# A transformer block on one core: a V tile moved behind transposes, rows normalised earlier, two lower pieces on another engine

## The chip, the cores and the metric

One core of a Trainium2 chip. The metric is device time in microseconds of one execution of the whole program, smaller is better; the median of several executions is quoted. Engines are TensorE (PE, with its weight loads PEld), VectorE (DVE), ScalarE (ACT), GpSimd (POOL) and SyncE (SP, which here only issues DMAs).

## The reference

An adaLN block over 2048 tokens of width 512 with 32 heads of 16, followed by an MLP of 1792:

```python
mod = (_silu(c) @ w_mod)                      # six rows of 512: sa, ca, ga, sb, cb, gb
h = _layernorm(x, axis=-1) * (1 + ca) + sa
qkv = h @ wqkv                                # 32 heads of 16
p = softmax(q k^T * scale)                    # 2048 x 2048 per head, no mask
x = x + ga * (p @ v) @ wo
h = _layernorm(x, axis=-1) * (1 + cb) + sb
x = x + gb * (gelu(h @ w1 + b1) @ w2 + b2)
```

All data are float32. The kernel keeps that precision by splitting each operand into an upper piece (rounded to fp32r) and a lower piece (the rest), and by multiplying three of the four products of pieces.

## The kernel before

**Order.** The kernel is scheduled by hand: each engine executes its instructions in the order in which the program emits them, and waits at an instruction until its inputs are there. A DMA is issued by the engine that the program names (`sy` is SP, `ac` is ScalarE), in that engine's order. The DMAs of both issuers share eight landing semaphores in rotation, so that an issue waits until the transfer that last used its semaphore has landed.

**First part (0 to about 83 us).** The tokens are four blocks of 512, each four tiles of 128 rows. `first_block` (L306) does block 0 with an order of its own: transposes, modulation rows in two halves (`mod_part`, L202, two groups of eight matmuls each), `mod_copy` to SBUF, `mod_cols` (L218: small matmuls that turn the row into a column scale and shift, modc), then the key and query projections of feature group 0, written as "hh", "lh" and "hl" (upper-upper, lower weights, lower activations) per chunk of 128 features. `put`, `value` and `lower` make the upper piece on ScalarE, the value on ScalarE and the lower piece on VectorE. Then the loop `for b in range(NB)` (L626) does, for each b: for b > 0 the statistics of block b + 1 (`ln1`, L271); the key projection of block b (`proj_qk`, w = 1); the query projection (w = 0); for b = 0 the statistics and rows of block 1; `V_A[b][0]` V tiles (`proj_v`, L470: 128 rows of V, 12 matmuls, one ScalarE evacuation, one store); the transposes of block b + 1 and their evacuation (`ln1_t`, L283: ScalarE makes h with modc, VectorE the upper piece, VectorE and GpSimd in turn the lower); `V_A[b][1]` V tiles; modulation rows. In `ln1` the statistics (L239 to L244: VectorE, and a GpSimd power for the factor) come first and the rows (L281, four VectorE instructions) only when the returned function is called.

**Key sums.** For feature groups 0 and 1, `proj_qk` of an odd block also forms the sum and the difference of its keys with those of the block before (VectorE L447), their upper pieces (ScalarE L448) and lower pieces (L463), and stores them (L453). These sums (`kpm_d`) serve a cheap bound of the row maxima. What `proj` calls last, `rest`, is the stores of the operation before: they are emitted one operation late, behind the next operation's evacuation.

**Second part.** V tiles not done yet and feature groups 1 to 3 form a list of items (`items`). From item FILL0 on, their matmuls are interleaved with "visits", three slots of row-maxima matmuls each (`half_slot`, L551: matmul L565, ScalarE L571, VectorE L574), which need the key sums in SBUF: `build_k` (L496) loads them, six DMAs for blocks 0 and 1 in the pass b = 3 of the first loop, the rest at fixed items. PSUM is eight banks; `bank()` hands out banks 3 to 6 in rotation in the first part.

**Third part.** Attention: score matmuls L966 and exponentials L967 with the products with V (L799), row maxima of later heads beside them (L546, L548); then output projection and MLP to the end.

## Time and profile before

| | us |
|---|---|
| median of 3 runs | 1738.33 (1737.28 to 1740.88) |
| profiled execution | 1736.68 |
| its span, first to last instruction | 1734.9 |
| TensorE busy in the span | 1726.3 (100%) |
| VectorE, ScalarE, GpSimd busy | 1393.7, 1352.0, 319.2 |

Rows below give start and length in microseconds, engine, line, operation and what it writes and reads; "x8" counts instructions that are merged in one row, whose starts follow one another; a bracket gives the idle time of the engine in front and what ended it. Matmuls are pipelined, so that a group's length reaches beyond the start of the next, and a busy share near 100% is no proof of a full TensorE; starts are compared instead. The granted TensorE clock is full throughout the span.

### The profile page before, as it was taken

The page shows a single profiled execution, that of the slowest core. Times are in us where ns is not written, and L with a number is a line of the kernel's source. Part 1 is how long each engine was busy: PE and PEld are TensorE (multiplying, and loading weights), DVE is VectorE, ACT ScalarE, POOL GpSimd, SP SyncE. Part 2 cuts the span into 40 slices and gives each one's busy share as a digit, 9 for nine tenths or more (in the row PEclk, how much of TensorE's full clock was granted, in tenths as well). Part 3 has the DMA queues.
Part 4 walks back from the last instruction along what each step waited for, and adds up shares of the span by engine and source line. Part 5 has one row for each costly group of instructions (what it writes and reads, how often), then busy time and mean ns, then how long its engine had stood idle before and what let it go on. Part 6 is the DMA issues. An engine that isn't in the chain of part 4 may idle for free.

```text
span 1734.9 us, 28894 instructions
## 1 busy us (share of the span) xinstructions
PE 1726.3 (100%) x10560; PEld 898.1 (52%) x10560; DVE 1393.7 (80%) x2558; ACT 1352.0 (78%) x2582; POOL 319.2 (18%) x346
## 2 busy tenths in 40 slices
PE   9999999999999999999999999999999999999998
PEld 6755554443433343343443443433333488888887
DVE  6599999898888888888888888888885296746553
ACT  4488888999999999999999999999999632222222
POOL 3205431010000000000000000000013154635562
PEclk9999999999999999999999999999999999999999
DMA  9767667412201400500500110101023064423331
GB/s 319 224 136 183 156 134 149 96 48 45 54 23 40 68 21 23 85 23 24 87 25 23 39 36 23 39 26 33 23 65 103 21 204 126 139 77 115 98 121 49
DMA packets 125218, 144.15 MB, mean 83 GB/s; under 512 B 39026, under 2 KB 74866, under 8 KB 123124
## 3 DMA queue, kind: packets, MB, share of 16 engines
q1 hardware_dynamic: 121764, 135.55, 30.8%
q10 hardware_dynamic: 3312, 6.76, 1.0%
q8 instruction: 83, 1.36, 0.3%
q14 instruction: 59, 0.48, 0.1%
HBM read 106.37 MB, written 35.87 MB: 82 GB/s over the span
## 4 chain that ended last, share of the span: by engine, by line
PE 97%; DVE 2%; DMA 0%; POOL 0%; ACT 0%; issue 0%; ACTq 0%; POOLq 0%
PE pv L799 29%; PE mx L546 20%; PE sc L303 16%; PE sc L966 13%; PE mx L1030 6%; PE mx L565 5%; PE pv L1030 2%; PE sc L906 2%; PE mx L906 1%; PE sc L260 0%; PE pv L343 0%; DMA qk<-parts 0%; PE sc L356 0%; DVE xin L281 0%; PE sc L205 0%; DVE glo L1013 0%
## 5 line engine op out<-in xcount | busy, mean ns | idle before, releaser
L967 ACT ACTIVATE p<-sc 128x512 f32<-128x512 f32 x2048 | 1054.7, 613 | 38.1 <-PE sc L966 12.0
L548 DVE TENSOR_REDUCE mxs<-mx 128x1 f32<-128x512 f32 x1472 | 927.2, 683 | 112.8 <-PE sc L966 84.8
L799 PE MATMUL pv<-p,vg 128*32 128x512 f32 x4096 | 546.0, 605 | 0.0
L966 PE MATMUL sc<-qst,kq 50*128 50x512 f32 x1024 | 284.2, 435 | 0.0
L966 PE MATMUL sc<-qst,kt 50*128 50x512 f32 x1024 | 282.1, 431 | 0.0
L546 PE MATMUL mx<-kq,qmx 48*128 48x512 f32 x768 | 261.8, 428 | 0.2
L546 PEld LDWEIGHTS mx<-kq,qmx 48*128 48x128 f32 x768 | 122.5, 184 | 228.4 <-DVE mxs L548 209.3
L546 PE MATMUL mx<-kt,qmx 48*128 48x512 f32 x704 | 239.9, 427 | 0.0
L546 PEld LDWEIGHTS mx<-kt,qmx 48*128 48x128 f32 x704 | 113.4, 184 | 208.5 <-DVE mxs L548 190.7
L1009 ACT ACTIVATE g<-sc,b_c 128x512 f32<-128x512 f32 x56 | 38.6, 690 | 222.7 <-PE sc L303 218.2
L574 DVE CUSTOM_DVE_ANT_0 cp<-mx,cp 128x512 f32<-128x512 f32 x288 | 182.8, 687 | 21.2 <-PE mx L565 17.3
L587 POOL CAST m<-mn 128x16 fp32r<-128x16 f32 x32 | 6.3, 198 | 1012.0 <-DVE mn L581 1011.9
L571 ACT ACTIVATE cp<-mx 128x512 f32<-128x512 f32 x288 | 151.5, 602 | 29.7 <-PE mx L565 29.3
L799 PEld LDWEIGHTS pv<-p,vg 128*32 128x32 f32 x4096 | 81.1, 108 | 180.6 <-issue 168.9
L966 PEld LDWEIGHTS sc<-qst,kq 50*128 50x128 f32 x1024 | 125.5, 185 | 32.2 <-ACT p L967 23.7
L1013 DVE TENSOR_TENSOR glo<-g,ghi 128x512 fp32r<-128x512 f32 x56 | 57.6, 1028 | 92.2 <-ACT ghi L1012 92.2
L966 PEld LDWEIGHTS sc<-qst,kt 50*128 50x128 f32 x1024 | 125.6, 185 | 9.8 <-ACT p L967 3.1
L835 POOL TENSOR_TENSOR w1l<-w1r,w1h 128x512 fp32r<-128x512 f32 x56 | 76.5, 1366 | 146.7 <-DVE w1h L834 123.1
L565 PE MATMUL mx<-kt,qmx 48*128 48x512 f32 x576 | 100.5, 437 | 0.0
L837 POOL TENSOR_TENSOR w2l<-w2r,w2h 128x512 fp32r<-128x512 f32 x56 | 82.5, 1473 | 6.2 <-DVE w2h L836 5.8
L565 PEld LDWEIGHTS mx<-kt,qmx 48*128 48x128 f32 x576 | 54.4, 184 | 49.4 <-DVE mxf L574 24.5
L303 PE MATMUL sc<-kt,w1h 128*128 128x512 f32 x224 | 73.9, 391 | 0.0
(175 smaller groups left out, 1667.7 us busy)
## 6 DMA issues: line engine op xcount, KB each, us to landing
w1r<-in_B_w_dram SPq DMA_DIRECT2D x56, 256.0 KB
w2r<-in_B_w_dram SPq DMA_DIRECT2D x56, 256.0 KB
qk<-parts SPq DMA_DIRECT2D x25, 512.0 KB
qmx<-qk SPq DMA_DIRECT2D x192, 64.0 KB
qst<-qk SPq DMA_DIRECT2D x192, 64.0 KB
kq<-qk SPq DMA_DIRECT2D x24, 256.0 KB
kt<-qk SPq DMA_DIRECT2D x24, 256.0 KB
vg<-v SPq DMA_DIRECT2D x8, 664.0 KB
```

Source lines behind the costliest of these rows:

```text
L303: te.matmul(ps, p, q, start=i == 0, stop=i == len(terms) - 1)
L546: te.matmul(ps, qmx[u][rows, p, qc * P : (qc + 1) * P], kst[u // NB][rows, p, kr * TB : (kr + 1) * TB], start=True, stop=True)
L548: ve.tensor_reduce(mxs[u][:, p, a, qc, kr : kr + 1], ps, axis=AX.X, op=ALU.max, negate=True)
L565: te.matmul(ps, qmx[u][rows, p, qc * P : (qc + 1) * P], kpm[u // NB][rows, p, t0 : t0 + TB], start=True, stop=True)
L571: ac.activation(vabs[n, a], ps, AF.Abs)
L574: ve.tensor_tensor_reduce(v, ps, v, -0.5, 3.0e38, ALU.add, ALU.min, mxs[u][:, p, a, qc, r : r + 1])
L799: te.matmul(cur_pv[0][32 * j : 32 * (j + 1)], vg[g][:, kc, j * VW : j * VW + 32], pt.pop((s, j)), start=kc == 0, stop=kc == NKC - 1)
L835: gp.tensor_tensor(alo, a, ahi.bitcast(F32), op=ALU.subtract)
L837: gp.tensor_tensor(blo, b, bhi.bitcast(F32), op=ALU.subtract)
L966: te.matmul(ps, k[r0 : r0 + KX, p, kc * P : (kc + 1) * P], q[r0 : r0 + KX, p], start=True, stop=True)
L967: ac.activation(pb, ps, AF.Exp, scale=SCALE)
L1030: te.matmul(acc[qb][t], p[:, sl], q, start=f == 0 and n == 0, stop=f == NF - 1 and n == 2)
```

## The change

- In `first_block`, the second modulation group is emitted before the second chunk's upper products, which move behind the copy of the modulation row; of the products with lower weights the first chunk's come before `mod_cols` and the second's behind it.
- `V_A[0]` is (3, 1): a fourth V tile is done in the pass b = 0, behind the transposes of block 1, and in front of the modulation rows. The remaining list of V tiles is one shorter; FILL0 and the item numbers at which loads are issued go down by one, so that they stay with the same V tile. The change of ScalarE's store queue to SP's at item 1 stays at item 1.
- `ln_stats` computes the factor for tiles 0 and 1, and for 2 and 3, separately.
- For b = 1 and 2 the rows of block b + 1 are normalised at once, in front of the key projection's evacuation.
- For b = 1 the stores of keys and key sums are emitted right behind the key projection, in front of the query projection.
- The lower pieces of block 0 and 1's key sums of group 0 are made by VectorE instead of GpSimd.

```diff
-FILL0 = 4
+FILL0 = 3
-V_A = ((3, 0), (1, 1), (0, 1))
+V_A = ((3, 1), (1, 1), (0, 1))
@@ ln_stats
+        rs = small.tile([P, 4], F32, tag="rs", name="rs")
         for t in range(4):
             ln_stat(mv, t, tiles[t])
-        rs = small.tile([P, 4], F32, tag="rs", name="rs")
-        ln_factor(mv, rs)
+            if t % 2:
+                ln_factor(mv, rs, t - 1, t + 1)
@@ first_block
         mm("hh", 0)
         mod_part(mod, 0, wms[0], HD, D)
-        mm("hh", 1)
         mod_part(mod, 1, wms[1], HD, D)
         value(0)
         mod_copy(mod, mrow, HD, D)
         value(1)
         lower(0)
-        mm("lh", 0, 1)
+        mm("hh", 1)
+        mm("lh", 0)
         mod_cols(0, mrow, cols, 2, 4)
+        mm("lh", 1)
         lower(1)
@@ proj_qk, rest
-                    eng = ve if not k and b == NB - 1 else gp
+                    eng = gp if k else ve
@@ for b in range(NB)
             if b + 1 < NB:
-                rows = ln1(b + 1)
+                xn = ln1(b + 1)()
...
-        elif b:
-            xn = rows()
+        elif b == 1:
+            rest()
+            rest = lambda: None
         proj(proj_qk, b, 0, 0, (), None if b else first[0])
@@ items
-        if 2 < n < 6:
-            build_k(kts[0], kpm_d[0], 0, 2 * TB, S, (n - 3,))
-        if n == 6:
+        if 1 < n < 5:
+            build_k(kts[0], kpm_d[0], 0, 2 * TB, S, (n - 2,))
+        if n == 5:
             load_w(2)
-        if n == 8:
+        if n == 7:
             build_k(kts[1], kpm_d[0], 1)
```

## The prediction

> **What bounds the kernel now.** First the page: its head, and the shares of the chain of work that ended last.

> ```profile
> span 1734.9 us, 28894 instructions
> ...
> PE 97%; DVE 2%; DMA 0%; POOL 0%; ACT 0%; issue 0%; ACTq 0%; POOLq 0%
> ```

> TensorE carries 97% of the chain, so a microsecond of TensorE idleness removed anywhere is worth one at the end, unless a later wait takes it back. The change touches the part before attention; there I read that chain in order of time, cut to 0–90 us.

> ```profile
> 25.57 6.75 DMA qk<-parts
> 32.40 0.34 ACTq L480
> ...
> 42.70 3.88 DVE xin L281 x4
> ...
> 48.26 2.80 PE sc L303 x12
> ...
> 70.64 12.33 PE sc L303 x52
> 82.97 0.66 PE mx L565 x3
> ```

> Columns are start, length, engine and line. In this stretch the chain leaves TensorE: a store of key pieces lands after 6.75 us, only then does ScalarE issue its next DMA (L480) and evacuate block 1's transposes (h); further on VectorE's row normalising (L281) holds block 2's. A V tile, 12 matmuls, is 2.80 us. From 70.64 it is TensorE alone: V tiles, then the first row-maxima matmuls (L565). What TensorE loses stands in its timeline:

> ```profile
> 30.58 1.51 PE L260 MATMUL mx<-ident,xin 128*128 128x128 f32 x12
> ...
> 32.46 1.92 PE L205 MATMUL sc<-wmod,s_m 128*32 128x512 f32 x16
> 34.31 2.02 PE L303 MATMUL sc<-hThi,w 128*128 128x512 f32 x6
> ...
> 39.22 2.00 PE L303 MATMUL sc<-hThi,w 128*128 128x512 f32 x8
> ...
> 45.66 2.16 PE L260 MATMUL mx<-ident,xin 128*128 128x128 f32 x12
> ...
> 48.02 2.11 PE L303 MATMUL sc<-wv,hThi 128*128 128x512 f32 x8
> ...
> 58.44 2.37 PE L260 MATMUL mx<-ident,xin 128*128 128x128 f32 x12
> ...
> 61.00 1.18 PE L303 MATMUL sc<-wv,hThi 128*128 128x512 f32 x4
> ```

> Matmul lengths overlap, so I take start to start. Block 1's key projection, also 12 matmuls, takes 39.22 − 34.31 = 4.91 where a V tile takes 2.80: **2.11 lost**, waiting for the evacuation of its transposes. Block 1's sixteen transposes take 32.46 − 30.58 = 1.88, block 2's 48.02 − 45.66 = 2.36 (**0.48 lost**), block 3's 61.00 − 58.44 = 2.56 (**0.68 lost**).

> **The change, part by part.** *Order of the first block.* The scale and shift of its last two chunks come through two modulation groups (L205), a copy and four small matmuls (L224).

> ```profile
> 14.99 0.73 PE L356 MATMUL sc<-hThi,w 128*128 128x512 f32 x2
> 15.66 0.64 PE L205 MATMUL sc<-wmod,s_m 128*32 128x256 f32 x8
> 16.23 1.20 PE L356 MATMUL sc<-hThi,w 128*128 128x512 f32 x4
> 17.26 0.50 PE L224 MATMUL pv<-sel,mrow 128*128 128x2 f32 x4
> ```

> The second group moves in front of two matmuls (15.66 − 14.99 = 0.67 earlier), and two of the four matmuls at 16.23 slip behind L224, (17.26 − 16.23) / 2 = 0.5. So L224 starts near 16.8 instead of 17.26, and the chain behind it (scale and shift, evacuation, lower piece, the next matmuls) follows up to 0.48 earlier. I take **0.35**, nearer the upper end since TensorE itself then becomes the limit; the lower end is 0 (the group's weights land later).

> *Fourth V tile.* It moves, 2.80 us with one ScalarE evacuation and one store, from in front of block 2's transposes to behind block 1's. The key projection then starts 2.80 − 0.35 after 34.31, at 36.8.

> ```profile
> 35.17 1.40 POOL L267 TENSOR_TENSOR hTlo<-h,hThi 128x512 fp32r<-128x512 f32 x1 [6.28 <-DVE hThi L266]
> 35.46 1.66 DVE L267 TENSOR_TENSOR hTlo<-h,hThi 128x512 fp32r<-128x512 f32 x1
> ...
> 37.05 0.41 DVE L266 CAST hThi<-h 128x512 fp32r<-128x512 f32 x1
> ```

> The last upper piece is there at 37.05 + 0.41 = 37.46 and is used by the seventh matmul, near 38.2. All **2.11** go. The list of V tiles shifts by one: three instead of four stand between block 3's projections and the first maxima visit, which stays in the eleventh V tile, since FILL0 and the item numbers fall by one.

> *Rows first, factor in halves, lower pieces on VectorE.* Each factor call gets one more VectorE instruction (0.17 and an estimated 0.1 of handover) and one more GpSimd power. Two GpSimd subtractions become two of VectorE.

> ```profile
> 28.92 1.92 DVE L281 TENSOR_SCALAR xin<-xin,mv,rs 128x512 f32<-128x512 f32 x4 [1.12 <-POOL rs L244]
> ...
> 40.77 0.68 DVE L441 TENSOR_TENSOR parts<-sc,parts 128x512 fp32r<-128x512 f32 x1
> ...
> 42.79 1.60 POOL L463 TENSOR_TENSOR pmh<-pm,pmh 128x512 fp32r<-128x512 f32 x1 [0.84 <-ACT pmh L448]
> ...
> 47.61 2.12 ACT L265 ACTIVATE h<-mx,modc 128x512 f32<-128x512 f32 x3 [0.74 <-PE mx L260]
> ...
> 55.52 0.17 DVE L243 TENSOR_SCALAR rs<-mv 128x4 f32<-128x4 f32 x1
> ...
> 58.64 0.60 ACT L440 ACTIVATE parts<-sc 128x512 fp32r<-128x512 f32 x1 [1.64 <-PE sc L303]
> ...
> 69.57 0.69 DVE L463 TENSOR_TENSOR pmh<-pm,pmh 128x512 fp32r<-128x512 f32 x1
> ```

> Four rows take 3.88 at 42.70, beside GpSimd's subtractions, and 1.92 at 28.92 without. VectorE in block 1 after the change: rows start where the key's lower piece did, 0.27 later, at 41.0, and end at 43.0; key lower piece and two sums, 42.70 − 40.77 = 1.93, to 44.9; two lower pieces of 0.69, to 46.3. Block 2's transposes come near 46.0 on TensorE and find their rows done: the **0.48** go. The price is on ScalarE. The stores of key and sums are now issued in front of the query's copy; behind the second sum's store (46.3) queue that copy (0.60), the query's lower piece on VectorE (0.68), the issue of its store and then h. With 0.34 an issue: 46.3 + 0.34 + 0.60 + 0.68 + 0.34 = 48.3, against 47.61: h **0.7 later**. The V tile behind the transposes takes the query's PSUM bank, free only at 47.9: a new TensorE wait, 0 to 0.4.

> The second power would run beside rows 0 and 1, as one does in the first block:

> ```profile
> 8.12 2.14 DVE L328 TENSOR_SCALAR xin<-xin,mv,rs 128x512 f32<-128x512 f32 x4
> ...
> 8.29 0.93 POOL L244 TENSOR_TENSOR rs<-rs,mhalf 128x2 f32<-128x2 f32 x1 [1.24 <-DVE rs L243]
> ```

> Four rows take 2.14 there instead of 1.92: 0.2 more, left to the range. [...]

> *Block 3.*

> ```profile
> 51.87 0.41 DVE L266 CAST hThi<-h 128x512 fp32r<-128x512 f32 x1
> ...
> 59.97 1.45 ACT L265 ACTIVATE h<-mx,modc 128x512 f32<-128x512 f32 x2 [0.74 <-PE mx L260]
> ...
> 65.07 1.28 POOL L267 TENSOR_TENSOR hTlo<-h,hThi 128x512 fp32r<-128x512 f32 x1 [1.42 <-DVE hThi L266]
> ```

> With h 0.7 later, block 2's last upper piece ends at 51.87 + 0.41 + 0.7 = 53.0; statistics and factor, which ended at 55.52 + 0.17, at 56.7; rows 1.92 later, at 58.6. Transposes want them from about 58.4: of 0.68 some 0.5 go. But the key's lower piece now stands behind the rows, to 59.3, and the issue of its store stands on ScalarE ahead of h: h near 59.7, against 59.97. So block 3's evacuation, and its last lower piece on GpSimd (65.07 + 1.28 = 66.35) that the key projection's last matmul uses, **stay about where they were**. TensorE arrives up to 0.4 sooner and waits.

> **What is late next.** Of 2.11 + 0.48 + 0.68 + 0.35 = 3.62 us lost, 3.2 to 3.4 go, and 2.80 of V tile are spent ahead of block 3. That pays only if the first visit really comes 3 us earlier. It needs blocks 0 and 1's key sums in SBUF (kt<-kpm), six loads that SP issues behind block 3's stores. SP's timeline, its waits between 82.2 and 82.9, and the last window (engines, clock, DMA share, GB/s):

> ```profile
> 71.43 4.86 SPq L496 DMA_DIRECT2D kt<-kpm  x6
> ...
> 82.61 0.82 SPq L480 DMA_DIRECT2D v<-vst  x2
> ```
> ```profile
> SPq L480 <- DMA kt<-kpm: 0.3, 1, 0.3
> ```
> ```profile
> 80.00:83.00 3.00, 3.00 (x15) 2.16 (x13) 0.00 (x0) 0.61 (x1) 0.00 (x0) 1.00 1.03 148
> ```

> SP's issue at 82.61 had waited for a kt load to land; the visit starts at 82.97, some 0.3 later. The DMA engines are full until then. These loads follow block 3's key projection, which does not move; the visit would be due near 79.8 and waits until 82.6. TensorE loses some 2.8 us there that it did not lose before.

> The sum on the path: 0.3 of slack at the loads, 0 from the evacuation chain in front of them: **−0.3 us**, 1736.4 for the profiled execution (1736.68, of which the span is 1734.9). The median of the runs shown, 1738.33, lies 1.65 above it; I apply the difference to the median: **1738.0**. Behind the first visit nothing changes in number or order.

> **Rivals.** (a) *The loads do not hold the visit*: their data land 3 us sooner. Then all but 0.2 of 3.62 reaches the end, −3.4, 1734.9. For it: nothing shows what the loads would do with fewer neighbours. Against: full DMA engines at 148 GB/s. [...] (b) *Slower: ScalarE stuck in a DMA issue.* At 32.40 it could issue a V store only when the transfer of 6.75 us had landed. Block 1 now has four such issues (V, key, two sums) in front of the query's copy; if one meets the semaphore of a transfer still under way, h, all of block 3's chain and the visit slip by the wait. It is slower from a wait of 0.3 us on; a transfer of 6.75 us that was issued 4.6 us before lands 2.1 late: +1.8, 1740.1. (c) *The evacuation chain shortens*: the V store at 32.40 meets another semaphore, and h of block 1, which follows it, starts up to a microsecond sooner. TensorE then bounds block 3's key projection, 0.4 sooner: −0.7, 1737.6.

> **How the numbers follow.** Forecast 0.55, (a) 0.15, (b) 0.15, (c) 0.15. 0.2% is 3.5 us, about what a measurement of this kernel can tell from no change; only the better half of (a), and a wait of 4 us in (b), get there, with a little for the scatter of the runs shown (1737.28 to 1740.88): faster 0.10, same 0.84, slower 0.06. The range takes in (a), (c), the forecast and most of (b): 1734.8 to 1739.8.

> **What would show it.** Right: block 1's key projection in 2.9 us; rows done before both sets of transposes; h of block 2 near 48.3 and of block 3 near 59.8; and at the first L565 a TensorE gap of 2 to 3 us with the kt loads landing at about the old time. Wrong: no gap there (rival a), or over 1 us of ScalarE idle ahead of block 1's query copy with a landing as its end (rival b).

## The result, and the profile after

The changed kernel takes **1748.01 us** (median of 12 executions, 1739.69 to 1758.32) against 1738.12 (1737.28 to 1740.88) for the kernel before: ratio 1.0055, 95% interval 1.0033 to 1.0077. It is slower by 9.9 us and scatters over 18.6 us instead of 3.6. The profiled execution took 1743.35. Its page, head and chain:

```profile
span 1741.6 us, 28898 instructions
...
PE 95%; DVE 2%; DMA 1%; ACT 0%; SPq 0%; POOL 0%; issue 0%; ACTq 0%
```

The span is 6.7 us longer, and DMA has entered the chain with 1%. The stall in block 1 that the V tile was to fill is filled (TensorE's timeline, after):

```profile
36.85 2.12 PE L304 MATMUL sc<-hThi,w 128*128 128x512 f32 x8
...
39.72 1.98 PE L304 MATMUL sc<-hThi,w 128*128 128x512 f32 x8
```

From 36.85 to 39.72 the key projection takes 2.87 us instead of 4.91. What came instead begins at the first visit (L567 here is L565 of before):

```profile
80.51 1.10 PE L304 MATMUL sc<-wv,hThi 128*128 128x512 f32 x4
83.34 0.47 PE L567 MATMUL mx<-kt,qmx 48*128 48x512 f32 x1 [1.73 <-DMA qmx<-qk]
83.96 0.80 PE L567 MATMUL mx<-kt,qmx 48*128 48x512 f32 x2 [0.16 <-DMA kt<-kpm]
84.69 2.07 PE L304 MATMUL sc<-wv,hThi 128*128 128x512 f32 x4
86.69 1.65 PE L567 MATMUL mx<-kt,qmx 48*128 48x512 f32 x6
...
94.83 1.19 PE L304 MATMUL sc<-wv,hThi 128*128 128x512 f32 x4
```

TensorE idles 1.73 us in front of the first visit. SP's timeline and its waits between 83 and 84 tell for what:

```profile
83.90 0.36 SPq L482 DMA_DIRECT2D v<-vst  x1
```
```profile
SPq L482 <- DMA kt<-kpm: 0.4, 1, 0.4
```

Again a kt load lands just before SP's V store (83.9; before: 82.6). The name in TensorE's bracket, qmx, is the transfer that ended nearest; kt is the one that both waits have in common, and e3 below moves its loads alone. Then look at the lengths: the four matmuls at 84.69 take 2.07 us where the four at 94.83 take 1.19. The windows of the same execution (length, engines with their counts, granted clock, DMA share, GB/s):

```profile
80.40:83.80 3.40, 1.67 (x7) 0.81 (x5) 0.00 (x0) 0.60 (x1) 0.00 (x0) 1.00 0.97 154
83.80:94.05 10.25, 10.09 (x29) 5.65 (x30) 3.84 (x12) 5.33 (x10) 0.00 (x0) 0.50 0.76 182
94.05:97.45 3.40, 3.40 (x18) 2.01 (x19) 2.85 (x9) 2.54 (x5) 0.00 (x0) 1.00 0.85 250
```

**Behind the wait the granted TensorE clock is 0.50 for 10.25 us.** In the timeline of before the same two V groups start here:

```profile
83.56 1.19 PE L303 MATMUL sc<-wv,hThi 128*128 128x512 f32 x4
...
89.75 1.18 PE L303 MATMUL sc<-wv,hThi 128*128 128x512 f32 x4
```

So the kernel is 84.69 − 83.56 = 1.13 us late when the clock falls and 94.83 − 89.75 = 5.08 late when it is back: 3.95 us are the clock's. This execution lies 4.7 us below the median; where the others lost their clock no trace shows. A smaller loss follows where attention starts, in after:

```profile
284.20 0.83 PE L969 MATMUL sc<-qst,kq 50*128 50x512 f32 x3 [0.77 <-ACT raw L435]
```

The first score matmul waits for ScalarE's evacuation of the last projection; before, no such wait stood there.

### The profile page after: what moved, and what is told of

Same layout as the page of the kernel before. It is cut to its first block, busy times and chain, and to the rows that moved or that the text cites. A ratio compares the mean times of both kernels' runs of the same rounds, so it can differ in the third digit from the quotient of the medians.

```text
span 1741.6 us, 28898 instructions
## 1 busy us (share of the span) xinstructions
PE 1729.5 (99%) x10560; PEld 900.4 (52%) x10560; DVE 1394.6 (80%) x2563; ACT 1351.9 (78%) x2582; POOL 317.4 (18%) x347
## 4 chain that ended last, share of the span: by engine, by line
PE 95%; DVE 2%; DMA 1%; ACT 0%; SPq 0%; POOL 0%; issue 0%; ACTq 0%
PE pv L802 29%; PE mx L548 20%; PE sc L304 15%; PE sc L969 14%; PE mx L1033 6%; PE mx L567 5%; PE pv L1033 2%; PE sc L909 2%; PE mx L909 1%; DMA qk<-parts 0%; PE sc L261 0%; DMA kt<-kpm 0%; PE sc L357 0%; DMA wmod<-in_w_mod_dram 0%; DVE mxs L550 0%; DMA v<-vst 0%
## 5 line engine op out<-in xcount | busy, mean ns | idle before, releaser
L969 PE MATMUL sc<-qst,kq 50*128 50x512 f32 x1024 | 284.0, 435 | 0.8 <-ACT raw L435 0.8
L969 PE MATMUL sc<-qst,kt 50*128 50x512 f32 x1024 | 282.4, 431 | 0.0
L969 PEld LDWEIGHTS sc<-qst,kq 50*128 50x128 f32 x1024 | 125.7, 185 | 32.9 <-ACT p L970 23.8
L969 PEld LDWEIGHTS sc<-qst,kt 50*128 50x128 f32 x1024 | 125.6, 185 | 10.0 <-ACT p L970 3.1
L567 PE MATMUL mx<-kt,qmx 48*128 48x512 f32 x576 | 102.4, 444 | 1.9 <-DMA qmx<-qk 1.7
L567 PEld LDWEIGHTS mx<-kt,qmx 48*128 48x128 f32 x576 | 55.3, 187 | 52.3 <-DVE mxf L576 25.6
```

What stands on the lines that cost most here:

```text
L567: te.matmul(ps, qmx[u][rows, p, qc * P : (qc + 1) * P], kpm[u // NB][rows, p, t0 : t0 + TB], start=True, stop=True)
L969: te.matmul(ps, k[r0 : r0 + KX, p, kc * P : (kc + 1) * P], q[r0 : r0 + KX, p], start=True, stop=True)
```

## Experiments

Medians below are of 5 to 12 executions, each ratio beside executions of the kernel before on the same chip (their medians: 1736.95 to 1738.23).

**e1_visit_later.**

```diff
-FILL0 = 3
+FILL0 = 4
```

> The changed kernel with FILL0 = 4 again: the visits start in the twelfth V tile instead of the eleventh, everything else as changed. Theory A (TensorE idles about 2 us at the first visit because the key sums' loads land late, and this idle time halves the granted clock for some 10 us or more): a V tile of 2.8 us covers the landing, no gap over 0.3 us at the first visit, mean clock 1.000, scatter of the runs back to that of before; the stalls removed in front show, since matmuls that were due at 82.9 in before come 1.4 us earlier: 1736.7 us (1736 to 1738). Theory B (the clock falls because of something else in the changed part, the gap is only beside it): clock still 0.99 to 0.998 and 1742 us or more.

Measured: 1738.14 us, ratio 1.0010 (1.0001 to 1.0018). TensorE's timeline and a window:

```profile
82.84 1.10 PE L304 MATMUL sc<-wv,hThi 128*128 128x512 f32 x4
83.86 0.73 PE L567 MATMUL mx<-kt,qmx 48*128 48x512 f32 x3
```
```profile
83.50:94.00 10.50, 10.50 (x51) 5.80 (x51) 7.37 (x23) 8.51 (x17) 0.00 (x0) 1.00 1.04 258
```

No gap, and in this execution full clock, as theory A has it; two of the eleven still have mean clocks of 0.997 and 0.995. The time expected was missed by 1.4 us: the visits start 0.96 later than in before (83.86 against 82.90), and the wait of 0.77 at the start of attention is still there (e12 takes it away).

**e2_filler.**

```diff
+NWARM2 = 10
...
+    def warm_up():
+        ps = bank_mx()
+        for _ in range(NWARM2):
+            te.matmul(ps[:, :P], ident, ident, start=True, stop=True)
...
-            fill = [lambda rest=rest: (rest(), visit())] + [visit] * (visits * (m + 1) // nm - visits * m // nm - 1)
+            fill = [lambda rest=rest, n=n: (rest(), warm_up() if n == FILL0 else None, visit())] + [visit] * (visits * (m + 1) // nm - visits * m // nm - 1)
```

> The changed kernel with ten transposing-size matmuls of the identity (2.2 us in all, result unused) put in front of the first visit, so that TensorE works while it would wait for the key sums. Theory A: the loads still land near 83.8, so the gap's own time stays (about 1 us against before at the first visit), but the clock stays at 1.000: 1739 to 1740 us with the scatter of before (3 us, not 19 us). Theory B: clock and time as in the changed kernel, 1742 us or more with the same wide scatter, or 2 us worse.

Measured: 1740.05 us, ratio 1.0021 (1.0009 to 1.0032); 7 of 11 executions at a mean clock of 0.999 or 1.000 where the changed kernel had 1 of 12. TensorE's timeline and a window:

```profile
82.29 2.39 PE L705 MATMUL mx<-ident 128*128 128x128 f32 x20
84.61 1.11 PE L568 MATMUL mx<-kt,qmx 48*128 48x512 f32 x3
```
```profile
84.60:94.00 9.40, 9.29 (x45) 5.17 (x44) 6.18 (x19) 7.33 (x14) 0.00 (x0) 1.00 1.01 253
```

The visit is even later than in the changed kernel (84.61 against 83.34), and yet the kernel is faster, by intervals that just do not overlap: work in place of the wait kept the clock at 1.00 here. This separates the clock from the wait. It is no cure for every execution: four of the eleven have mean clocks of 0.994 to 0.998, and this one has 0.999.

**e3_early_kt.**

```diff
             load_qm(0)
+            build_k(kts[0], kpm_d[0], 0, 0, 2 * TB)
...
             rest, st[0] = lambda: None, ac
-            build_k(kts[0], kpm_d[0], 0, 0, 2 * TB)
```

> The changed kernel with the six loads of the key sums of blocks 0 and 1 issued right behind the first load of queries, in front of block 3's key and key sum stores, instead of behind them. Theory A: the loads land by 75 us, no gap at the first visit, clock 1.000, and the stalls removed in front show in full: 1736.7 us (1735.5 to 1738). Theory B: clock below 0.998 all the same, 1742 us or more.

Measured: 1737.18 us, ratio 1.0000 (0.9991 to 1.0008). TensorE's timeline, and the windows at the start of attention:

```profile
81.55 0.73 PE L567 MATMUL mx<-kt,qmx 48*128 48x512 f32 x3
```
```profile
281.00:284.40 3.40, 3.40 (x16) 1.31 (x15) 1.78 (x3) 2.15 (x5) 0.00 (x0) 0.50 0.96 246
```

The first visit comes at 81.55, 1.35 before that of the kernel before, without a gap: here the gain of the change is seen. In this execution it is lost again where attention starts: the first scores wait 0.77 us, as in the changed kernel, and 3.4 us from 281 on run at half clock.

**e4_before_visit_early.**

```diff
 # the kernel before
-FILL0 = 4
+FILL0 = 3
```

> The kernel before with FILL0 = 3 and nothing else of the change: the visits start in the tenth V tile, 2.8 us earlier, and the key sums land near 82.5 as before. Theory A: TensorE waits about 2.4 us at the first visit, the clock is halved there for about 10 us, which costs some 4 us more: 1743 to 1745 us, mean clock 0.99 to 0.998, wide scatter. Theory B: the wait alone, 1739 to 1741 us at clock 1.000.

Measured: 1757.61 us (1750.15 to 1769.07), ratio 1.0127 (1.0096 to 1.0158), some three times the loss that theory A had named. TensorE's timeline and windows:

```profile
82.94 0.47 PE L565 MATMUL mx<-kt,qmx 48*128 48x512 f32 x1 [1.46 <-issue]
...
141.52 0.94 PE L565 MATMUL mx<-kt,qmx 48*128 48x512 f32 x4 [3.40 <-DMA qmx<-qk]
```
```profile
84.00:111.30 27.30, 27.30 (x78) 15.20 (x76) 13.45 (x42) 13.14 (x26) 0.00 (x0) 0.50 0.40 111
111.30:142.00 30.70, 27.30 (x135) 16.48 (x135) 25.78 (x82) 23.38 (x45) 0.42 (x2) 1.00 0.61 114
142.00:159.10 17.10, 17.10 (x51) 9.04 (x48) 9.98 (x32) 8.71 (x17) 2.31 (x4) 0.50 0.23 78
```

A visit before its data is enough, with no other part of the change. Two waits, of 1.46 and 3.40 us, are each followed by a stretch at half clock, of 27.3 and 17.1 us.

**e5_early_kt_ring.**

```diff
 # e3_early_kt
-    set_rings(sc=(0, 2, 3, 1), mx=(4, 5, 6), pv=(7,))
+    set_rings(sc=(1, 2, 3, 0), mx=(4, 5, 6), pv=(7,))
```

> e3_early_kt with the order of the score banks changed from 0, 2, 3, 1 to 1, 2, 3, 0 at the start of attention. Theory C (with one V tile fewer the list of items has 33 instead of 34 entries, the last one ends in PSUM bank 0 instead of 1, and the first score matmul, which is given bank 0, waits for its evacuation; the 0.8 us of idle there let the clock fall for 3.4 us): no gap over 0.5 us at the start of attention, the 1.3 us gained at the first visit stay to the end: 1736.0 us, 1.3 below before. Rival: the loss at 277 to 284 us has another cause and stays, 1737.2 us as in e3_early_kt.

Measured: 1735.73 us, ratio 0.9994 (0.9985 to 1.0002), no execution below 0.999. TensorE's timeline at the start of attention:

```profile
276.06 1.20 PE L304 MATMUL sc<-hTlo,w 128*128 128x512 f32 x4
277.19 0.50 PE L969 MATMUL sc<-qst,kq 50*128 50x512 f32 x2
```

The scores (L969) follow the projection with no wait. So far theory C holds: the item list's odd length had put the last projection into the bank of the first score. The time is 1.2 us below before, near the 1.3 expected, but the interval reaches 1. That the idle time lowered the clock there, the other half of theory C, is not shown, and it is not needed: in e6, which has this order too and no wait, the clock falls to 0.50 at 280.33 all the same (last section).

**e6_early_kt_ring_no_store.**

```diff
 # e5_early_kt_ring
-        elif b == 1:
-            rest()
-            rest = lambda: None
```

> e5_early_kt_ring without the early emission of block 1's key and key sum stores (the branch elif b == 1 left out, so they come behind the query's evacuation as before the change). Theory D (the four DMA issues in a row on ScalarE in front of the query copy hold that copy, the V tile behind block 2's transposes waits 1.4 us for the query's bank, and block 3's evacuation comes late): this gap and those in block 3's key projection go, the first visit comes 2.7 to 3.2 us earlier than in before, 1734.5 us. Rival: the query copy waits for something else, or block 3 is held by the rows that now stand in front of the key's lower piece; then no more than 0.5 us below e5_early_kt_ring.

Measured: 1736.67 us, ratio 0.9999 (0.9991 to 1.0008). ScalarE's part of its timeline:

```profile
48.28 0.60 ACT L480 ACTIVATE vst<-sc 128x512 f32<-128x512 f32 x1 [2.56 <-PE sc L261]
49.71 0.37 ACTq L458 DMA_DIRECT2D qk<-parts  x1
...
50.13 2.12 ACT L266 ACTIVATE h<-mx,modc 128x512 f32<-128x512 f32 x3 [1.24 <-DMA v<-vst]
```

The first half of theory D holds: the query copy is early again, and the V tile behind block 2's transposes starts at 47.85 with no wait. The second half falls: h of block 2 starts at 50.13 as with the early stores, since now the issue of the query store (49.71) waits until a V store has landed, and the first visit comes only 0.16 us before that of e5 (81.64 against 81.80).

**e7_no_early_store.** The edit of e6 on the changed kernel alone:

```diff
-        elif b == 1:
-            rest()
-            rest = lambda: None
```

> The changed kernel without the early emission of block 1's stores, and with the late loads of the key sums. Theory A: block 3's chain and the landing come 1 to 1.5 us earlier, but TensorE is due 1.4 us earlier too, so the gap at the first visit stays near 2 us and the clock falls all the same: 1742 to 1752 us with wide scatter. Rival (the early stores alone make the change slow): 1737 to 1738 us at clock 1.000.

Measured: 1741.45 us (1738.34 to 1756.39), ratio 1.0041 (1.0021 to 1.0062); 6 of 12 executions below 0.999. Windows of its profiled execution (1746.71 us):

```profile
84.90:88.30 3.40, 3.40 (x11) 1.93 (x10) 1.92 (x6) 1.57 (x3) 0.00 (x0) 0.51 1.09 258
88.30:282.90 194.60, 193.82 (x925) 113.12 (x924) 184.43 (x589) 163.45 (x316) 68.46 (x86) 1.00 0.65 151
282.90:300.00 17.10, 17.10 (x65) 6.34 (x64) 9.08 (x16) 9.79 (x21) 0.57 (x1) 0.50 0.97 141
```

The early stores are not what makes the change slow. The median lies just under what was expected, for the clock fell in half of the executions only; in this one it fell at both waits.

**e8_v_tile_only.** The V tile's lines of the change alone:

```diff
 # the kernel before
-FILL0 = 4
+FILL0 = 3
...
-V_A = ((3, 0), (1, 1), (0, 1))
+V_A = ((3, 1), (1, 1), (0, 1))
...
-        if 2 < n < 6:
-            build_k(kts[0], kpm_d[0], 0, 2 * TB, S, (n - 3,))
-        if n == 6:
+        if 1 < n < 5:
+            build_k(kts[0], kpm_d[0], 0, 2 * TB, S, (n - 2,))
+        if n == 5:
...
-        if n == 8:
+        if n == 7:
```

> The kernel before with the fourth V tile behind block 1's transposes (V_A, FILL0 and the item numbers) and nothing else of the change. Theory A: block 1's key projection loses its 2.1 us of waiting, the rows still hold the transposes of blocks 2 and 3, the key sums land at 82.5 to 83.5 as before while the visit is due near 81, so a gap of 2 us and a halved clock: 1742 to 1755 us, wide scatter. Rival (the other parts are needed for the loss): 1736 to 1738 us.

Measured: 1741.69 us, ratio 1.0027 (1.0016 to 1.0038). TensorE's timeline, and ScalarE's part of the timeline in block 2:

```profile
84.70 0.47 PE L565 MATMUL mx<-kt,qmx 48*128 48x512 f32 x1 [1.91 <-issue]
```
```profile
46.51 3.93 ACTq L453 DMA_DIRECT2D kpm<-pmh  x2
...
50.49 0.61 ACT L478 ACTIVATE vst<-sc 128x512 f32<-128x512 f32 x1 [5.54 <-DMA v<-vst]
...
51.01 2.12 ACT L265 ACTIVATE h<-mx,modc 128x512 f32<-128x512 f32 x3
```

The V tile alone brings the gap (1.91) and the loss, with a median just under what was expected. In this execution the clock stayed full, against theory A, and the span is 1738.0, 3.1 above before: the loss without the clock. It shows too where the loads get late: h of block 2 starts at 51.01 instead of 47.61, behind a ScalarE that stood 5.54 us at the issues of the key sums, until a V store had landed.

**e9_rows_first.**

```diff
 # e5_early_kt_ring
+        if b == 0:
+            mrow = mod_rows(wms)
+            wms = [load_wm(2, 0), load_wm(5, 1)]
         for _ in range(V_A[b][1]):
             proj(proj_v, *vitems.pop(0))
-        if b < 2:
+        if b == 1:
             mrow = mod_rows(wms)
-        if b == 0:
-            wms = [load_wm(2, 0), load_wm(5, 1)]
```

> e5_early_kt_ring with block 1's modulation rows (L205) in front of the moved V tile instead of behind it, so that the two weight loads and the four x loads that wait for them are issued near 33.7 us as before the change, not at 36. Theory E (the moved V tile delayed these loads by 2.5 us, the stores of V, keys and sums then stand behind them in the DMA engines, and ScalarE's issue of the query store waits for the V store's landing, with h of block 2 behind it): h of block 2 starts near 48.5 instead of 50.3, the 1.4 us gap of TensorE behind block 2's transposes shrinks below 0.7, and the first visit comes 1.8 to 2.6 us before that of the kernel before: 1734.8 us. Rival (the four stores issued in a row, or the rows in front of the key's lower piece, hold h): as e5_early_kt_ring, 1735.7.

Measured: 1736.14 us beside 1738.23, ratio **0.9987 (0.9979 to 0.9996)**. The loads and ScalarE in its timeline, the loads in that of the changed kernel:

```profile
32.81 1.24 SPq L145 DMA_DIRECT2D wmod<-in_w_mod_dram  x2
...
47.31 0.60 ACT L442 ACTIVATE parts<-sc 128x512 fp32r<-128x512 f32 x1 [2.20 <-DMA v<-vst]
...
49.07 2.12 ACT L266 ACTIVATE h<-mx,modc 128x512 f32<-128x512 f32 x3 [0.68 <-DVE modc L227]
```
```profile
36.12 1.24 SPq L145 DMA_DIRECT2D wmod<-in_w_mod_dram  x2
```

The loads leave 3.3 us earlier and h comes at 49.07, 1.2 before that of e5 (50.27), from which it differs in this alone, and 1.0 before the changed kernel's 50.03, though 0.6 after what was expected. Theory E explains part; the four issues in a row still hold the query copy until 47.31. The first visit comes at 80.56, 2.3 us before that of before. This version and the next are the only ones whose interval lies below 1.

**e10_rows_first_no_store.**

```diff
 # e9_rows_first
-        elif b == 1:
-            rest()
-            rest = lambda: None
```

> e9_rows_first without the early emission of block 1's key and key sum stores. Theory E: with the loads early again, the order of the stores decides little; the query copy leaves earlier, so that the gap behind block 2's transposes goes altogether and h of block 2 starts near 48: 1734.5 us, at most 0.5 us from e9. If the row of four issues was a second cause of its own, it is 1 us or more below e9.

Measured: 1736.48 us, ratio 0.9988 (0.9979 to 0.9997), 0.3 us from e9: with the loads early, the place of the stores decides nothing that can be measured.

**e11_gap_no_visits.**

```diff
-FILL0 = 3
+FILL0 = 5
...
+    def probe():
+        for a in range(2):
+            r = slice(a * 64, a * 64 + KR)
+            te.matmul(bank_mx(), qmx[0][r, 0, :P], kts[0][r, 0, TB : 2 * TB], start=True, stop=True)
...
+        if n == 3:
+            fill = [lambda rest=rest: (rest(), probe()), lambda: None, lambda: None]
...
-    set_rings(sc=(0, 2, 3, 1), mx=(4, 5, 6), pv=(7,))
+    set_rings(sc=(1, 2, 3, 0), mx=(4, 5, 6), pv=(7,))
```

> The changed kernel with FILL0 = 5, so that the visits start in the thirteenth V tile, the score banks in the order 1, 2, 3, 0, and two matmuls in the eleventh V tile that only read the key sums (result unused) where the first visit was: TensorE waits there for the loads as in the changed kernel, but full V tiles of 128 rows follow for some 5 us, instead of visits of 48 rows. If the wait alone lowers the clock: half clock from about 84 us on in most executions, 1739 to 1750 us. If the thin matmuls of the visits behind the wait are needed to lower it or keep it low: clock 0.999 to 1.000, at most one stretch of 3.4 us, 1737 to 1739 us.

Measured: 1745.57 us, ratio 1.0047 (1.0034 to 1.0060), mean clocks 0.998 to 1.000. TensorE's timeline and a window:

```profile
83.14 0.47 PE L704 MATMUL mx<-kt,qmx 48*128 48x512 f32 x1 [1.51 <-DMA qmx<-qk]
```
```profile
84.00:94.00 10.00, 10.00 (x44) 6.76 (x45) 1.56 (x5) 4.36 (x8) 0.00 (x0) 1.00 0.99 253
```

A wait of 1.51 us, and the clock stays at 1.00 with V tiles of 128 rows behind it. In five executions this speaks for the second reading (thin matmuls behind the wait are needed), though the wait is also 0.2 shorter than in the changed kernel. The time is no verdict on the clock: this execution, at full clock, has a span 6.2 us above that of before. The visits start two V tiles later; that this is what costs the 6 us is likely but not shown, and neither reading had named it.

**e12_later_ring.**

```diff
-FILL0 = 3
+FILL0 = 4
...
-    set_rings(sc=(0, 2, 3, 1), mx=(4, 5, 6), pv=(7,))
+    set_rings(sc=(1, 2, 3, 0), mx=(4, 5, 6), pv=(7,))
```

> e1_visit_later with the score banks in the order 1, 2, 3, 0: the smallest repair of the change. Theories A and C: no gap at the first visit and none at the start of attention, so the 0.3 to 0.8 us that e1_visit_later lies above before go: within 0.5 us of before, and above e5_early_kt_ring by about 1 us since the visits start later. Rival: something else costs e1_visit_later its time, and it stays 0.8 us above before.

Measured: 1737.73 us, ratio 0.9998 (0.9989 to 1.0007): as expected, the change's loss is gone with two constants. One of its twelve executions took 2089.71 us at a mean clock of 0.735; the ratio is without it.

## Why the prediction was wrong

**Right.** The stalls that the change aimed at went as worked out: block 1's projection in 2.87 us (2.9 forecast, start 36.85 against 36.8), block 2's rows done long before their transposes. The forecast's main point also held: the first visit waits for the key sums' loads. e1, e3 and e4 show it from three sides. Its sign came only in part: the gap was 1.73 us where 2 to 3 were named, and the loads landed 1.3 us later than before, not at the old time. The first block's 0.35 was 0.2: block 1's transposes start at 30.35 in after, 30.58 before.

```profile
30.35 1.47 PE L261 MATMUL mx<-ident,xin 128*128 128x128 f32 x12
```

**Wrong, the step that decided.** "TensorE loses some 2.8 us there that it did not lose before" priced the wait at its own length. The wait of 1.73 us was followed by 10.25 us at half clock, 3.95 us more in the profiled execution, and by more than that in six of the eleven others (mean clocks down to 0.988), which makes the median. e2 puts work into the wait and keeps the clock there; e4 makes the wait alone and loses 20 us. The page of before showed a full clock throughout (PEclk 9 in all 40 slices), so its rows could not price this; the DMA engines, full (a share of 1.03) until 0.3 us before the first visit, showed where a wait would stand, not what would follow it.

**Wrong in size: ScalarE in block 2.** "46.3 + 0.34 + 0.60 + 0.68 + 0.34 = 48.3" for h took every issue at 0.34 us. ScalarE in the changed kernel:

```profile
45.28 0.33 ACTq L482 DMA_DIRECT2D v<-vst  x1
45.70 0.39 ACTq L458 DMA_DIRECT2D qk<-parts  x1
...
46.19 1.84 ACTq L455 DMA_DIRECT2D kpm<-pmh  x2
...
48.08 0.60 ACT L442 ACTIVATE parts<-sc 128x512 fp32r<-128x512 f32 x1 [2.23 <-DMA v<-vst]
...
50.03 2.12 ACT L266 ACTIVATE h<-mx,modc 128x512 f32<-128x512 f32 x3 [0.86 <-DVE modc L227]
```

The two sum issues take 1.84 us instead of 0.7 (the trace of before already had a key store's issue of 0.80, at 43.27), the query copy starts at 48.08, and h at 50.03: 1.7 later than worked out. This is the mechanism of rival (b), with 1.7 of its 2.1 us, and its sign stands in the row at 48.08: over 1 us of idle with a landing as its end. It moved block 3's chain, which the forecast held in place (h at 61.44, 59.7 forecast), and the loads (83.9 instead of 82.6) with it. TensorE pays at once, too: the V tile behind block 2's transposes, for which a wait of 0 to 0.4 was forecast, waits 1.40 us for the query's bank.

```profile
49.45 2.14 PE L304 MATMUL sc<-wv,hThi 128*128 128x512 f32 x8 [1.40 <-DVE parts L443]
```

So TensorE came to the first visit 1.4 us earlier than before (80.51 against 81.88 for the group in front) instead of 3.1, and left it 1.13 late instead of 0.3 early, before the clock had cost anything. The cause of the long issues was only half seen: the moved V tile also stands in front of the modulation rows, so that 2 MB of weight loads, which wait for those rows, left at 36.12 instead of 33.6, and the stores stood behind them. e9 takes that back, and of the 1.7 h gains 1.0.

**Missed.** The list of items became odd, and the last projection and the first score share a PSUM bank: 0.77 us at 284, shown by e5. The forecast had said that behind the first visit nothing changes in number or order.

**Open.** Why the clock, once low, stays so for one step of 3.4 us in e7, three in the changed kernel and eight in e4, with nearly the same work in each (3.2, 2.8 and 2.9 matmuls a microsecond), is not shown. When it falls is not shown either: the last section has what stood in front of some of the falls.

## What to carry to other kernels

The gap of 1.73 us in front of matmuls of 48 rows was not priced by its length, since the 10.25 us at half clock behind it cost 3.95 us more: look up the granted clock in windows behind every wait of TensorE, and put other work (e2), or the loads (e3), in front of it before a schedule is moved forward. When work is moved between two stages, list what the later stage's first instruction reads, and when it lands in the trace; and count the list that it is taken from, since ring positions behind it shift by one (here the PSUM banks, for 0.77 us).

## What the hardware showed

**What stands in front of the falls.** In the changed kernel TensorE works 1.67 of the 3.40 us in front of the fall at 83.80. The windows below are of e4, in front of the fall at 84.00 (1.30 of 3.00 us), and of e11 and e8, around their waits of 1.51 and 1.91 us (1.26 of 3.00 and 0.29 of 2.20):

```profile
81.00:84.00 3.00, 1.30 (x6) 0.43 (x4) 0.00 (x0) 0.74 (x2) 0.00 (x0) 1.00 0.97 154
...
81.00:84.00 3.00, 1.26 (x5) 0.55 (x3) 0.00 (x0) 0.34 (x1) 0.00 (x0) 1.00 0.93 160
...
82.50:84.70 2.20, 0.29 (x2) 0.03 (x1) 0.00 (x0) 0.00 (x0) 0.00 (x0) 1.00 1.00 129
```

In e11 and e8 the clock stays at 1.00 behind them (84.00 to 94.00, 84.70 to 95.00), so the idle time alone did not decide it. Nor does the fall in e6 follow a wait: TensorE is busy for 3.41 of 3.41 us at the start of attention, most of it with the scores of 50 rows and the maxima of 48, and the next 3.42 us run at 0.50.

```profile
276.92:280.33 3.41, 3.41 (x18) 1.81 (x19) 3.21 (x10) 3.07 (x7) 2.03 (x4) 1.00 0.03 7
280.33:283.75 3.42, 3.42 (x17) 1.31 (x15) 1.80 (x3) 2.18 (x5) 0.22 (x1) 0.50 0.69 194
```

That the length of a wait and the rows of the matmuls around it count together is an estimate from e2, e6 and e11, and not shown.

**Issue times.** Four DMA issues in a row on ScalarE (45.28 to 48.03 in the changed kernel) took 0.33, 0.39, 0.47 and 1.27 us, with the DMA engines' share at 1.09. The query copy, queued behind them, started at 48.08; why the last took longest is not shown.
